# Loads of q, k and v: four chunks on odd partitions, buffers of their own, k's exp in one operation

## The chip, the cores and the metric

The kernel runs on one core of one Trainium2 chip. The metric is the time of one execution on the device in microseconds (us), lower is better. The profile's span is shorter than that time, because it begins at the first and ends at the last instruction. A run gives several timed executions and the profile of one of them. A fast execution that took 1 us or more longer than others of its kernel is called a long one below.

## The reference, cut to what matters

Linear attention with two softmaxes, then a gated feed-forward block:

```python
def _attn_ref(q, k, v):                       # each (8, 8, 576, 64) float32
    q_s = np.exp(q - np.max(q, axis=-1, keepdims=True))
    q_s = q_s / (np.sum(q_s, axis=-1, keepdims=True) + 1e-09)
    k_s = np.exp(k - np.max(k, axis=2, keepdims=True))
    k_s = k_s / (np.sum(k_s, axis=2, keepdims=True) + 1e-09)
    kv = np.einsum('bhsd,bhse->bhde', k_s, v)
    return np.einsum('bhsd,bhde->bhse', q_s, kv)

def _moe_ref(x, w_gate, w_val, w_out):        # x (4608, 512), d_ff 1536
    g = x @ w_gate
    gelu = 0.5 * g * (1.0 + erf(g * inv_sqrt2))
    return gelu * (x @ w_val) @ w_out
```

## The kernel before

A sequence of 576 rows is 64 groups of 9 rows. A partition pair shares a group: the even partition takes rows 0 to 4 (five chunks of 64 numbers per head), the odd one rows 4 to 8. Row 4 is thus loaded twice, and its copy on the odd partitions must not count: k's exp for that chunk is a second operation with a bias of -1e30 on the odd partitions, so that exp gives zero there.

```python
tiny = const.tile([P, 1], f32)
nc.vector.memset(tiny, 0.0)
kbias = const.tile([P, 1], f32)               # -1e30 on odd partitions
nc.vector.reduce_sum(kbias, ident.rearrange("p (m t) -> p t m", t=2)[:, 1, :], ...)
nc.vector.tensor_scalar(out=kbias, in0=kbias, scalar1=-1e30, scalar2=None, op0=ALU.mult)
... # ek, eq, v16, xtr, q0r, eq0r, weights follow in the same pools

def load(src, nm, b, h0, h1, n0):             # ldp: five buffers in rotation
    key = (nm, b)
    if key not in tiles:
        tiles[key] = ldp.tile([P, H, NC * D], f32, name=f"{nm}t", tag="ld")
    for t in range(2):
        nc.sync.dma_start(
            out=tiles[key][t:P:2, h0:h1, n0 * D:NC * D],
            in_=src[b, h0:h1].rearrange("h (m n) d -> m h (n d)", n=NT)[
                :, :, (4 * t + n0) * D:(4 * t + NC) * D])

... # the order of the loads, all on one queue
for src, nm, n0 in ((q, "q", 1), (k, "k", 0), (v, "v", 0)):
    load(src, nm, 0, 0, H, n0)
for c in range(NW):
    load_w_gv(c)                              # gate and value weights
for c in range(3):
    load_w_o(c)                               # output weights
load(q, "q", 1, 0, H, 0)
for c in range(3, NO):
    load_w_o(c)
```

The weights arrive as float32 in staging tiles and are cast to float16 on GpSimd. Between the feed-forward groups of a batch, the attention of the next batch is worked in by a plan: `at(batch, FI or NS, index, ...)` hangs work behind a gate/value group (FI) or an output tile (NS).

The softmax here doesn't subtract the row's maximum and nothing guards it: scores larger than these inputs give would overflow.

## Time and profile before

| | before |
|---|---|
| time, median of 3 | 324.06 us |
| the execution that was profiled | 325.62 us (span 323.8) |
| TensorE busy | 98% |
| spacing of 512-column matmul starts | 216 ns |
| v of batch 0 landed | 15.40 us |
| first feed-forward matmul | 19.07 us |
| last output weights landed | 43.91 us |

The prediction shows the page's lines for this kernel. These two rows of the windows view of the kernel before give, for 22 to 43 us and for 43 to 49 us: the length, busy time of TensorE, its weight loads, VectorE, ScalarE and GpSimd with counts, the granted clock, the DMA share and GB/s.

```profile
22.00:43.00 21.00, 21.00 (x99) 9.57 (x98) 8.20 (x12) 10.18 (x14) 13.03 (x14) 1.00 1.07 394
43.00:49.00 6.00, 5.88 (x34) 2.84 (x33) 5.27 (x10) 3.22 (x5) 3.89 (x4) 1.00 1.06 393
```

The reader is to see that the transfers run at full occupation through this whole stretch while TensorE works on what they bring. TensorE waits almost nowhere, but nothing in the row says by how much each transfer is early.

### The profile page before, as it was taken

The page shows a single profiled execution, that of the slowest core. Times are in us where ns is not written, and L with a number is a line of the kernel's source. Part 1 is how long each engine was busy: PE and PEld are TensorE (multiplying, and loading weights), DVE is VectorE, ACT ScalarE, POOL GpSimd, SP SyncE. Part 2 cuts the span into 40 slices and gives each one's busy share as a digit, 9 for nine tenths or more (in the row PEclk, how much of TensorE's full clock was granted, in tenths as well). Part 3 has the DMA queues.
Part 4 walks back from the last instruction along what each step waited for, and adds up shares of the span by engine and source line. Part 5 has one row for each costly group of instructions (what it writes and reads, how often), then busy time and mean ns, then how long its engine had stood idle before and what let it go on. Part 6 is the DMA issues. An engine that isn't in the chain of part 4 may idle for free.

```text
span 323.8 us, 4510 instructions
## 1 busy us (share of the span) xinstructions
PE 315.9 (98%) x1670; PEld 150.9 (47%) x1670; DVE 189.9 (59%) x339; ACT 142.7 (44%) x189; POOL 43.1 (13%) x58
## 2 busy tenths in 40 slices
PE   8799999999999999999999999999999999999995
PEld 3344445445445444444444444444454444444444
DVE  2654366498569758945795579647963433333431
ACT  4463476698353492238433842384321133103310
POOL 1267552303000300030003000300000000000000
PEclk9999999999999999999999999999999999999999
DMA  6999999990178004941495139512021110040002
GB/s 217 356 324 389 401 396 390 392 357 7 67 235 316 2 11 167 387 117 29 139 381 149 22 125 366 176 31 95 36 50 31 67 65 0 4 108 21 0 34 97
DMA packets 47718, 53.12 MB, mean 164 GB/s; under 512 B 11344, under 2 KB 43472, under 8 KB 47696
## 3 DMA queue, kind: packets, MB, share of 16 engines
q1 hardware_dynamic: 47552, 52.77, 47.2%
q8 instruction: 13, 0.21, 0.3%
q10 hardware_dynamic: 144, 0.07, 0.1%
q14 instruction: 9, 0.07, 0.1%
HBM read 40.76 MB, written 9.44 MB: 155 GB/s over the span
## 4 chain that ended last, share of the span: by engine, by line
PE 86%; ACT 3%; DMA 3%; issue 2%; DVE 2%; SPq 1%; POOL 0%; DVEq 0%; ACTq 0%; POOLq 0%
PE psg L305 27%; PE psv L305 27%; PE psy L349 26%; DMA vt<-in_v_dram 3%; PE pskv L200 3%; PE psx L283 2%; ACT L149 1%; SPq L103 1%; ACT eq L149 1%; PE psl L370 1%; ACT L310 1%; PE pst L226 1%; DVE kv_sb L208 0%; DVE rq L166 0%; ACT gl L310 0%
## 5 line engine op out<-in xcount | busy, mean ns | idle before, releaser
L310 ACT ACTIVATE gl<-psg 128x512 f32<-128x512 f32 x108 | 63.9, 598 | 120.2 <-PE psg L305 118.9
L312 DVE SCALAR_TENSOR_TENSOR ht<-psv,gl 128x512 f16<-128x512 f32 x108 | 73.0, 683 | 66.7 <-PE psv L305 62.3
L305 PE MATMUL psg<-xt,wg_sb 128*128 128x512 f16 x384 | 100.6, 379 | 0.1
L305 PE MATMUL psv<-xt,wv_sb 128*128 128x512 f16 x384 | 100.2, 379 | 0.1
L349 PE MATMUL psy<-wo_sb,ht 128*128 128x512 f16 x420 | 94.7, 379 | 0.0
L305 PEld LDWEIGHTS <-wv_sb 128*128 128x128 f16 x432 | 42.3, 98 | 51.8 <-issue 1.0
L349 PEld LDWEIGHTS <-ht 128*128 128x128 f16 x420 | 40.8, 98 | 47.8
L305 PEld LDWEIGHTS <-wg_sb 128*128 128x128 f16 x432 | 41.3, 98 | 46.7 <-issue 1.4
L398 DVE TENSOR_SCALAR yo<-psy 128x512 f32<-128x512 f32 x30 | 20.6, 689 | 34.6 <-PE psy L349 34.6
L125 POOL CAST v<-vt 128x640 f16<-128x640 f32 x26 | 18.3, 743 | 141.8 <-DMA vt<-in_v_dram 108.4
L166 DVE TENSOR_REDUCE rq<-eq 128x10 f32<-128x640 f16 (+1 forms) x32 | 25.3, 791 | 10.4 <-ACT eq L149 10.0
L173 DVE TENSOR_TENSOR eq<-eq,rrq 128x640 f16<-128x640 f16 (+1 forms) x28 | 23.4, 836 | 0.4
L127 ACT CAST xt<-psx 128x512 f16<-128x512 f32 x19 | 10.3, 588 | 27.3 <-PE psx L283 27.3
L149 ACT ACTIVATE eq<-qt 128x2560 f16<-128x2560 f32 (+1 forms) x9 | 18.3, 2049 | 4.2 <-DMA qt<-in_q_dram 4.1
L149 ACT ACTIVATE ek<-kt 128x2048 f16<-128x2048 f32 (+1 forms) x10 | 15.6, 1558 | 6.4 <-DMA kt<-in_k_dram 6.4
L297 PE MATMUL pswarm<-warm,ident 128*128 128x512 f16 x46 | 12.6, 435 | 1.4 <-POOL ident masks.py:199 1.4
L249 DVE STREAM_TRANSPOSE et<-eq 128x640 f16<-128x640 f16 x16 | 13.5, 845 | 0.6
L200 PE MATMUL pskv<-v,ek 128*128 128x130 f16 x160 | 11.8, 220 | 1.9 <-DVE v L129 1.9
L200 PEld LDWEIGHTS <-ek 128*128 128x128 f16 x160 | 10.3, 97 | 5.5 <-ACT v L127 2.4
L305 PE MATMUL psg<-xtr,wg_sb 128*128 128x512 f16 x48 | 12.3, 379 | 0.5 <-ACT xtr L127 0.5
L305 PE MATMUL psv<-xtr,wv_sb 128*128 128x512 f16 x48 | 12.3, 379 | 0.0
L283 PE MATMUL psx<-eqt,kv_sb 128*128 128x512 f16 x32 | 10.2, 381 | 0.3 <-DVE eqt L129 0.2
(57 smaller groups left out, 134.5 us busy)
## 6 DMA issues: line engine op xcount, KB each, us to landing
kt<-in_k_dram SPq DMA_DIRECT2D x14, 640.0 KB, 8.0
vt<-in_v_dram SPq DMA_DIRECT2D x14, 640.0 KB, 10.0
qt<-in_q_dram SPq DMA_DIRECT2D x14, 640.0 KB, 6.0
out_dram<-yo SPq DMA_DIRECT2D x14, 512.0 KB, 3.1
wost<-in_moe_w_out_dram SPq DMA_DIRECT2D x6, 512.0 KB, 7.9
wgst<-in_moe_w_gate_dram SPq DMA_DIRECT2D x5, 512.0 KB, 7.5
wvst<-in_moe_w_val_dram SPq DMA_DIRECT2D x5, 512.0 KB, 7.5
eqt<-et SPq DMA_DIRECT2D x64, 40.0 KB, 2.0
```

Source lines behind the costliest of these rows:

```text
L125: nc.gpsimd.tensor_copy(out=dst, in_=src)
L149: nc.scalar.activation(out=dst[:, c0:c1, h0 * D:h1 * D].rearrange("p n (h d) -> p h n d", d=D), in_=tiles[(nm, b)][:, h0:h1, c0 * D:c1 * D ...
L166: nc.vector.reduce_sum(rq, e, axis=mybir.AxisListType.X)
L173: (nc.gpsimd if eng == "pool" else nc.vector).tensor_tensor(out=e, in0=e, in1=rrq.unsqueeze(-1).to_broadcast((P, n, 2, D)), op=ALU.mult)
L200: nc.tensor.matmul(pskv[:, j, :], ek_b[b % 2][:, n, hp * P:(hp + 1) * P], v16_b[b % 2][:, n, 2 * hp:2 * hp + 2, 0:VW], start=(n == 0), sto ...
L249: nc.vector.transpose(out=et[:, hp].rearrange("p c (n i) -> p n c i", i=32), in_=eq_b[b % 2][:, :, hp * P:(hp + 1) * P].rearrange("p n (c ...
L283: nc.tensor.matmul(psx, st[(b, "kv", hp)].rearrange("p h e -> p (h e)"), xq(b, hp), start=True, stop=True)
L305: nc.tensor.matmul(ps, w[:, ci, fi * P:(fi + 1) * P], xt[:, ci, :], start=(ci == 0), stop=(ci == HP - 1))
L310: nc.scalar.activation(out=gl, in_=psg, func=ACTF.Gelu)
L312: nc.vector.scalar_tensor_tensor(out=ht, in0=psv, scalar=_H_SCALE, in1=gl, op0=ALU.mult, op1=ALU.mult)
L349: nc.tensor.matmul(psy, hts[fi][:, ns * P:(ns + 1) * P], wo_sb[:, fi, :], start=(fi == 0), stop=(fi == NFI - 1))
L398: nc.vector.tensor_scalar(out=yo, in0=psy, scalar1=1.0 / _H_SCALE, scalar2=None, op0=ALU.mult)
```

## The change

It saves the double load of row 4: odd partitions load four chunks. The unused fifth chunk then has to hold a constant (zero for q and v, -1e30 for k, whose exp is zero). So q, k and v get fixed buffers, filled once, and k's exp becomes one operation without a bias. Some loads and units move to other places of the plan. The core of the diff:

```diff
-    ldp = ctx.enter_context(tc.tile_pool(name="ldp", bufs=5))
...
     tiny = const.tile([P, 1], f32)
     nc.vector.memset(tiny, 0.0)
-    kbias = const.tile([P, 1], f32)
-    nc.vector.reduce_sum(kbias, ident.rearrange("p (m t) -> p t m", t=2)[:, 1, :], ...)
-    nc.vector.tensor_scalar(out=kbias, in0=kbias, scalar1=-1e30, scalar2=None, op0=ALU.mult)
...
+    ld_b = {}
+    for nm, n, fill in (("k", 2, -1e30), ("v", 1, 0.0), ("q", 2, 0.0)):
+        ld_b[nm] = []
+        for i in range(n):
+            t = const.tile([P, H, NC * D], f32, name=f"{nm}t{i}")
+            (nc.vector if i == 0 else nc.gpsimd).memset(t[:, :, 0:D], fill)
+            ld_b[nm].append(t)
...
-        for t in range(2):
+        tiles[(nm, b)] = ld_b[nm][b % len(ld_b[nm])]
+        for t, c0 in ((0, n0), (1, 1)):
             nc.sync.dma_start(
-                out=tiles[key][t:P:2, h0:h1, n0 * D:NC * D],
+                out=tiles[(nm, b)][t:P:2, h0:h1, c0 * D:NC * D],
...
-        for c0, c1 in parts if nm == "k" else ((n0, NC),):
-            nc.scalar.activation(out=..., in_=..., func=ACTF.Exp,
-                bias=kbias[:, 0:1] if c1 == 1 else 0.0)
+        nc.scalar.activation(out=..., in_=..., func=ACTF.Exp)
...
-    at(1, FI, 7, L(exp, "k", 2, 0, H, 0, ((1, NC),)), L(cast_v, 2, 0, H))
+    at(1, FI, 7, L(exp, "k", 2, 0, 4), L(cast_v, 2, 0, H))
...
-                at(b, NS, 3, L(unit_xrem, n))
+                at(b, NS, 12, L(unit_xrem, n))
...
-                mm_out(psy, hts, ns, range(NFI))
+                mm_out(psy, hts, ns, range(NFI // 2))
+                ride(b, NS, 10 + ns)
+                mm_out(psy, hts, ns, range(NFI // 2, NFI))
```

More of the change, by code (lines that the diff above doesn't have):

```diff
@@ L74 @@
     nc.vector.memset(tiny, 0.0)
-    kbias = const.tile([P, 1], f32)
-    nc.vector.reduce_sum(kbias, ident.rearrange("p (m t) -> p t m", t=2)[:, 1, :],
-                         axis=mybir.AxisListType.X)
-    nc.vector.tensor_scalar(out=kbias, in0=kbias, scalar1=-1e30, scalar2=None, op0=ALU.mult)
     ek_b, eq_b, v16_b = [], [], []
@@ L98, in load @@
     def load(src, nm, b, h0, h1, n0):
-        key = (nm, b)
-        if key not in tiles:
-            tiles[key] = ldp.tile([P, H, NC * D], f32, name=f"{nm}t", tag="ld")
-        for t in range(2):
+        tiles[(nm, b)] = ld_b[nm][b % len(ld_b[nm])]
+        for t, c0 in ((0, n0), (1, 1)):
             nc.sync.dma_start(
-                out=tiles[key][t:P:2, h0:h1, n0 * D:NC * D],
+                out=tiles[(nm, b)][t:P:2, h0:h1, c0 * D:NC * D],
                 in_=src[b, h0:h1].rearrange("h (m n) d -> m h (n d)", n=NT)[
-                    :, :, (4 * t + n0) * D:(4 * t + NC) * D])
+                    :, :, (4 * t + c0) * D:(4 * t + NC) * D])
     wst = {}
@@ L142, in cast_w_o, with exp @@
         copy_on(eng, wo_sb[:, 2 * c:2 * c + 2, :], wst[("wo", c)])
-    def exp(nm, b, h0=0, h1=H, n0=0, parts=((1, NC), (0, 1))):
+    def exp(nm, b, h0=0, h1=H, n0=0):
         dst = (ek_b if nm == "k" else eq_b)[b % 2]
-        for c0, c1 in parts if nm == "k" else ((n0, NC),):
-            nc.scalar.activation(
-                out=dst[:, c0:c1, h0 * D:h1 * D].rearrange("p n (h d) -> p h n d", d=D),
-                in_=tiles[(nm, b)][:, h0:h1, c0 * D:c1 * D].rearrange("p h (n d) -> p h n d", d=D),
-                func=ACTF.Exp, bias=kbias[:, 0:1] if c1 == 1 else 0.0)
+        nc.scalar.activation(
+            out=dst[:, n0:NC, h0 * D:h1 * D].rearrange("p n (h d) -> p h n d", d=D),
+            in_=tiles[(nm, b)][:, h0:h1, n0 * D:NC * D].rearrange("p h (n d) -> p h n d", d=D),
+            func=ACTF.Exp)
     def cast_v(b, h0, h1, eng="pool"):
@@ L414, with load_batch @@
         load_w_o(c)
-    for h0 in (0, 4):
-        load(k, "k", 1, h0, h0 + 4, 0)
-        load(v, "v", 1, h0, h0 + 4, 0)
-    def load_batch(b):
-        for src, nm in ((q, "q"), (k, "k"), (v, "v")):
+    def load_batch(b, what=((q, "q"), (k, "k"), (v, "v"))):
+        for src, nm in what:
             load(src, nm, b, 0, H, 0)
-    load_batch(2)
-    nc.sync.dma_start(out=q0r, in_=q[0].rearrange("h (m n) d -> m h (n d)", n=NT)[:, :, 0:D])
     preload(ACTF.Exp)
@@ L441 @@
     cast_v(0, 6, 8, "dve")
+    for h0 in (0, 4):
+        load(k, "k", 1, h0, h0 + 4, 0)
+        load(v, "v", 1, h0, h0 + 4, 0)
+    load_batch(2, ((q, "q"), (k, "k")))
+    nc.sync.dma_start(out=q0r, in_=q[0].rearrange("h (m n) d -> m h (n d)", n=NT)[:, :, 0:D])
     warm_pe(2)
@@ L471 @@
     at(0, NS, 5, L(unit_t, 1, 0))
-    at(0, NS, 16, L(unit_kv, 1, 0), L(cast_v, 1, 4, 8))
+    at(0, NS, 16, L(unit_kv, 1, 0), L(cast_v, 1, 4, 8), L(load_batch, 2, ((v, "v"),)))
     at(0, NS, 6, L(norm, 1, 3))
@@ L484 @@
     at(1, FI, 6, L(norm, 2, 3))
-    at(1, FI, 7, L(exp, "k", 2, 0, H, 0, ((1, NC),)), L(cast_v, 2, 0, H))
+    at(1, FI, 7, L(exp, "k", 2, 0, 4), L(cast_v, 2, 0, H))
     at(1, FI, 9, L(unit_t, 2, 0))
     at(1, FI, 10, L(unit_t, 2, 1))
-    at(1, FI, 11, L(load_batch, 3), L(exp, "k", 2, 0, H, 0, ((0, 1),)),
-       L(exp, "q", 3), L(exp, "k", 3), L(exp_rem0), L(cast_v, 3, 0, H))
+    at(1, FI, 11, L(load_batch, 3), L(exp, "k", 2, 4, 8), L(exp, "q", 3), L(exp, "k", 3), L(exp_rem0), L(cast_v, 3, 0, H))
     at(1, NS, 0, L(unit_trem, 2), L(unit_kv, 2, 0))
-    at(1, NS, 1, L(unit_x, 2, 0, "dve"), L(unit_kv, 2, 1))
+    at(1, NS, 1, L(unit_x, 2, 0, "dve"))
+    at(1, NS, 12, L(unit_kv, 2, 1))
     at(1, NS, 2, L(unit_x, 2, 1, "dve"), L(unit_x, 2, 2, "dve"))
```

## The prediction

> **What bounds the kernel now.** I read the page first, for the shares of the engines:
>
> ```profile
> PE 315.9 (98%) x1670; PEld 150.9 (47%) x1670; DVE 189.9 (59%) x339; ACT 142.7 (44%) x189; POOL 43.1 (13%) x58
> ```
>
> TensorE has work in 315.9 of 323.8 us and no other engine reaches 60%. That busy figure flatters it, since the records overlap: one 512-column matmul is recorded as 379 ns, but in the trace's order of time the starts lie 216 ns apart. So I looked for the places where starts lie further apart. Next the waits, for TensorE alone:
>
> ```profile
> PE pskv L200 <- DVE v L129: 1.9, 1, 1.9
> PE pswarm L297 <- POOL ident masks.py:199: 1.4, 1, 1.4
> PE psg L305 <- ACT xtr L127: 0.5, 1, 0.5
> PE psx L283 <- DVE eqt L129: 0.2, 1, 0.2
> ```
>
> There are four waits, 4.0 us in all, and only the first and third can concern this change. Third, the chain that ended last, cut to the first 24 us:
>
> ```profile
> 4.23 0.04 issue
> 4.27 11.13 DMA vt<-in_v_dram
> 15.40 0.03 issue
> ...
> 15.50 0.84 DVE v L129
> 16.34 0.14 issue
> 16.48 0.75 PE pskv L200 x10
> ```
>
> Up to 15.40 us the end of the kernel hangs on one thing: the second half of batch 0's v landing (issue at 4.27, landing 11.13 later). Then VectorE casts it, TensorE makes k'v, and at 19.07 us the feed-forward stream begins. From there I compared starts of neighbouring matmuls. Beyond the regular spacing there are only some 2.2 us of gaps in 300 us. The ones over 0.15 us lie at 19.1, 50.7, 52.2, 55.0, 66.5, 73.3, 89.9 and 257.2 us. Two of them bear on the change. At 73.3 us, the timelines of TensorE and of ScalarE:
>
> ```profile
> 72.66 1.02 PE L305 MATMUL psg<-xt,wg_sb 128*128 128x512 f16 x4
> 73.80 1.02 PE L305 MATMUL psv<-xt,wv_sb 128*128 128x512 f16 x4
> ```
>
> ```profile
> 68.64 1.28 ACT L149 ACT_TABLE_LOAD   x1
> 69.93 1.91 ACT L149 ACTIVATE ek<-kt 128x2048 f16<-128x2048 f32 x1
> 71.86 1.28 ACT L310 ACT_TABLE_LOAD   x1
> 73.15 1.09 ACT L310 ACTIVATE gl<-psg 128x512 f32<-128x512 f32 x2
> ```
>
> The psv group should start 0.86 us after the psg group, at 73.52; it starts at 73.80. ScalarE was away from the Gelus for 4.5 us with k's exp between two table loads. The six PSUM buffers ran full, and one came free when the Gelu of 73.15 ended (about 73.75). At 257.2 us:
>
> ```profile
> 257.13 0.28 PE L290 MATMUL psxr<-eqt,kv_sb 128*128 128x64 f16 x4
> 257.87 1.02 PE L305 MATMUL psg<-xtr,wg_sb 128*128 128x512 f16 x4 [0.46 <-ACT xtr L127]
> ```
>
> Here the remainder rows of the last batch are made and copied by ScalarE directly before the tile that reads them. The gap is 652 ns in place of 216.
>
> **What the Trainium skill says.** "DMA: Bandwidth & Descriptors", section "Why small descriptors are slow (HBM only)", gives each packet a fixed overhead besides its bytes. The trace agrees: the median packet took 27 ns with 512 bytes, 46 with 1024 and 55 with 1280. So cutting 256 bytes of 1280 saves 9 ns of 55, 16% and not 20%. "ScalarE: Activation LUTs", section "What ACT_TABLE_LOAD costs", gives an ACTIVATE with immediate bias 186 ns + 0.833 ns per element, and 93 ns more with a bias in memory. The trace has 2.34 us for 2560 elements (formula 2.32) and 1.28 us for a table load (page 1.283), so it agrees. "VectorE: DVE Perf Modes", section "Zero memsets can be issued as uint32 (trn2)", has one cycle per element for a memset; 512 elements took 0.48 us here and 256 took 0.27, which agrees.
>
> **The change part by part.**
>
> 1. Fewer bytes. An odd-partition load has 64 partitions x 8 heads = 512 packets, 32 on each of 16 DMA engines. 32 x 9 ns = 0.29 us less per tensor and batch. Ahead of v's landing lie two such loads that change (k0 and v0; q0 loaded four chunks already): 2 x 0.29 = 0.58 us. The landings of v0's odd half on the 16 engines run from 12.83 to 15.40 us, with the 15th at 14.47. One engine is late: one of its packets took 1156 ns at 6.9 us, and it works off its last v packets 52 ns apart. A lagging engine drains the same 64 changed packets, so it also gains 0.58 us, unless the odd slow packet falls otherwise. v lands near 14.82. Nothing else should then be late. The q chain on VectorE is done by 13.04. k0 also lands 0.29 earlier, near 11.8, and its two exps (part 4) end near 14.4. The gate weights follow v in the same queue and shift with it; their casts on GpSimd were 1.3 us ahead at fi 2. So the matmul start moves from 16.48 to about 15.9. On the path: -0.58 us.
>
> 2. The same saving for later tensors (about 11 x 131 KB up to batch 3) ends the busy stretch of DMA, full until about 73 us, some 3 us sooner. TensorE waits for no transfer after 19 us, so this is worth 0.
>
> 3. Constants and buffers. VectorE loses kbias (two operations, 0.36 us, plus a wait for the identity), and gets three memsets of 512 elements, estimated at 0.55 us each from the rows above; GpSimd gets two. The even half of k0 must wait for k's memset, which I put at 2.8 us: constants until 1.75, eq0r 0.48, k 0.55. It was issued at 2.24. The transfer does not notice: the first k packet ran only at 5.56, behind q, and the first packets came 1.55 us after q's issue, so an issue at 2.85 would be ready by 4.4. q0 loads chunks 1 to 4 only, which its memset doesn't touch. Worth 0.
>
> 4. k's exp as one operation. Per half tensor 1.06 + 0.49 less overlap = 1.45 us becomes 1.26 us (the cast of 1280 elements on ScalarE takes 1.26); per whole tensor 2.5 becomes 2.34. ScalarE is 44% busy, so only one place counts: at FI 7 of batch 1 the exp of 1.91 us becomes a half exp of 1.26. The Gelus return 0.65 us sooner, more than the 0.28 us gap at 73.3, which closes: -0.28 us. The other half goes behind the last Gelu of the batch (1.26 for 0.72 us), where ScalarE is wanted by nobody until 89 us.
>
> 5. Moved work. The remainder rows go from behind the fourth output tile to the middle of the third, 1.3 + 2.6 us before their reader. The gap of 652 - 216 ns closes: -0.44 us. unit_kv(2, 1) moves to mid-tile, because its exp is now later; VectorE needs about 0.8 us for its two kv_sb, and the rest of the tile is 6 x 216 ns = 1.3 us. Worth 0.
>
> Sum: -0.58 - 0.28 - 0.44 = -1.30 us. 324.06 becomes 322.8 us (-0.4%).
>
> **Rivals.**
>
> *A wait takes the place of the one removed.* v has one buffer now, so v of batch 2 cannot be asked for before GpSimd has cast v of batch 1 (51.79 to 53.17 us before), and the queue behind it (stores, batch 3) stands still meanwhile. For it: SyncE issues in order, and v2 was issued at 49.24 before. Against: v2's four casts ended at 64.87 and are read at 79.64, 15 us of slack, and an asking at 52 with 2 us of latency and 3.3 us of transfer lands near 57 to 58. It would have to be very wrong; then some 1 to 3 us lost, 324 to 326.
>
> *The memsets hold up the start.* If q0's load waited for q's own memset (the third on VectorE, near 3.8 us), every first transfer would start 3 us later: 325.5 to 326. Against: the parts touched are disjoint. Even then it stays inside 2%.
>
> *The prologue's gain is lost or doubled by the late engine.* The stall of 1156 ns is one packet of one engine. If it falls elsewhere, v can land at 14.0 (-1.5 us) or, with a second such packet, not earlier at all. That makes 321.9 to 323.4, and it is my main uncertainty.
>
> *A PSUM pair is too short at the new place of the remainder rows.* They reuse the buffer of unit_x 0, freed by VectorE (in batch 3 at 152.9 us); the new place comes at 151.88 + 1.30 = 153.2. The margin is only 0.3 us. If it fails, batches 3 to 6 lose 0.1 to 0.3 us each: up to 1 us back, 323.8.
>
> **Range and chances.** Central 322.8. All three gains hold and the late engine vanishes: 321.6. Prologue gain lost and part of the PSUM margin too: 323.9. Two per cent is 6.5 us; all gaps after 19 us plus the wait before the first k'v make 4.5 us, so faster by 2% is practically out (0.01). Slower by 2% needs a stall that I have not seen (0.01). Within: 0.98.
>
> **What would show it.** In the chain of waits the vt transfer should end near 14.8, and k'v start near 15.9 us. If it ends there and the first feed-forward matmul does not come 0.58 us sooner, the weights or ScalarE have become the limit. The row "psg waits for xtr" should be gone from TensorE's waits. In the middle of batch 1 the psg and psv starts should be 0.86 us apart, with an exp of 128x1280 near 1.26 us before. Each k load should still have its first packet directly behind q's. A wait of psxr on VectorE, of pskv on v in batch 2, or a first q issue after 3 us would make the prediction wrong.

## The result

| | before | after |
|---|---|---|
| median | 324.2 us (324.0 to 324.4, 4 executions) | 325.88 us (325.70 to 326.02, 4 executions) |
| ratio after/before | | 1.0052, 95% interval 1.0034 to 1.0069 |

The change makes the kernel 0.5% slower, and the output is correct. That is within the 2% that the prediction expected, but on the other side of zero. Here and below, a ratio is the mean time of one kernel's fast executions over the mean of the other's in the same rounds, so it isn't quite the ratio of the medians that are quoted.

The first line to look at is the DMA queue: packets, megabytes, share of the time of 16 engines. Before:

```profile
q1 hardware_dynamic: 47552, 52.77, 47.2%
```

After:

```profile
q1 hardware_dynamic: 47552, 49.75, 48.1%
```

The same number of packets carries 6% fewer bytes and keeps the engines busy for longer. Fewer bytes with more time means that the packets themselves have become slower. The windows view of the kernel after shows when that mattered (columns as above):

```profile
22.00:43.00 21.00, 20.96 (x98) 9.32 (x97) 7.46 (x11) 8.07 (x12) 12.08 (x12) 1.00 1.07 364
43.00:49.00 6.00, 4.03 (x21) 1.67 (x18) 4.24 (x8) 3.49 (x3) 3.50 (x4) 1.00 1.08 357
```

At the same share, the rate fell from 394 to 364 GB/s, and directly afterwards TensorE stood still for 2 of 6 us. The waits of TensorE in the kernel after (total us, times, longest) name who kept it:

```profile
PE psy L348 <- POOL wo_sb L126: 1.1, 2, 0.8
PE pst L225 <- POOL eq L172: 1.0, 1, 1.0
```

Neither wait is in the trace of the kernel before that the prediction read; a long execution of that kernel (a1, below) has the second, with 0.7 us. Both name GpSimd, but GpSimd is only the middle of the story. The chain of waits of the kernel after (start, length, what) leads back from the second of them to a transfer:

```profile
31.16 9.68 DMA qt<-in_q_dram
...
40.89 1.28 ACT L148
...
42.19 2.35 ACT eq L148
...
44.56 0.83 DVE rq L165
...
47.87 1.27 POOL eq L172
...
49.19 0.40 PE pst L225 x4
```

The q of batch 1 lands at 40.84 us; ScalarE's table load and exp start that moment, VectorE sums, GpSimd multiplies, and TensorE's transposes wait for it. The other wait has the same root by another way: GpSimd's casts of the output weights wait for their transfers. GpSimd's timeline in the kernel after (start, length, engine, line, what, idle time before and its releaser):

```profile
43.60 1.04 POOL L126 CAST wo_sb<-wost 128x1024 f16<-128x1024 f32 x1 [0.31 <-DMA wost<-in_moe_w_out_dram]
44.96 1.04 POOL L126 CAST wo_sb<-wost 128x1024 f16<-128x1024 f32 x1 [0.32 <-DMA wost<-in_moe_w_out_dram]
```

and TensorE beside it, where each bracket is a stall:

```profile
44.69 0.59 PE L348 MATMUL psy<-wo_sb,ht 128*128 128x512 f16 x2 [0.37 <-POOL wo_sb L126]
46.06 1.89 PE L348 MATMUL psy<-wo_sb,ht 128*128 128x512 f16 x8 [0.77 <-POOL wo_sb L126]
47.78 0.39 PE L225 MATMUL pst<-ident,eq 128*128 128x128 f16 x4
49.19 0.40 PE L225 MATMUL pst<-ident,eq 128*128 128x128 f16 x4 [1.02 <-POOL eq L172]
```

Counted as excess over the regular 216 ns between neighbouring starts, the three stalls are 0.53, 0.93 and 1.02 us, 2.49 us in all.

The two gaps that the change was to close did close. At 73 us the psg and psv groups of the kernel after start 0.86 us apart:

```profile
73.65 1.02 PE L304 MATMUL psg<-xt,wg_sb 128*128 128x512 f16 x4
74.51 1.03 PE L304 MATMUL psv<-xt,wv_sb 128*128 128x512 f16 x4
```

and the tile of the remainder rows of the last batch starts with no wait:

```profile
255.37 2.75 PE L348 MATMUL psy<-wo_sb,ht 128*128 128x512 f16 x12
257.96 1.03 PE L304 MATMUL psg<-xtr,wg_sb 128*128 128x512 f16 x4
```

So the question for the experiments was why packets became slower. The addresses in the two compiled kernels suggested an answer. The small tile `kbias` takes one 32-byte slot on each partition. It stood ahead of nearly everything else, so that without it every later tile lies 32 bytes lower. Before, the targets of the loads (q, k, v and the weights' staging tiles) began at multiples of 256 bytes, for example 93440 and 144640; after, all begin 224 past one, for example 56544 and 144608.

### The profile page after: what moved, and what is told of

It is laid out like the page before. It is cut to its first block, busy times and chain, and to the rows that moved or that the text cites. A ratio compares the mean times of both kernels' runs of the same rounds, so it can differ in the third digit from the quotient of the medians.

```text
span 323.9 us, 4499 instructions
## 1 busy us (share of the span) xinstructions
PE 316.4 (98%) x1670; PEld 150.6 (47%) x1670; DVE 191.1 (59%) x340; ACT 141.0 (44%) x180; POOL 44.8 (14%) x60
## 3 DMA queue, kind: packets, MB, share of 16 engines
q1 hardware_dynamic: 47552, 49.75, 48.1%
## 4 chain that ended last, share of the span: by engine, by line
PE 81%; DMA 8%; SPq 3%; ACT 2%; DVE 2%; issue 1%; POOL 1%; ACTq 0%; DVEq 0%; POOLq 0%
PE psy L348 26%; PE psg L304 25%; PE psv L304 24%; DMA wgst<-in_moe_w_gate_dram 5%; DMA qt<-in_q_dram 3%; PE pskv L199 2%; SPq L120 2%; PE psx L282 2%; ACT eq L148 1%; PE psl L369 1%; SPq L104 1%; ACT L148 1%; PE pst L225 1%; POOL wg_sb L126 1%; DVE rq L165 0%
## 5 line engine op out<-in xcount | busy, mean ns | idle before, releaser
L148 ACT ACTIVATE ek<-kt 128x1280 f16<-128x1280 f32 (+1 forms) x11 | 19.1, 1746 | 4.3 <-DMA kt<-in_k_dram 4.3
```

The costliest lines, as they stand in the source:

```text
L148: nc.scalar.activation(out=dst[:, n0:NC, h0 * D:h1 * D].rearrange("p n (h d) -> p h n d", d=D), in_=tiles[(nm, b)][:, h0:h1, n0 * D:NC * D ...
```

## The experiments

The theory: a DMA whose SBUF target does not start on a multiple of 256 bytes takes longer per packet, the loads up to 45 us come later by it, and TensorE waits. The rivals: the new order of loads or the fixed buffers delay them; k's exp or the moved units cost time; the difference is spread between executions. The means of packet times below are taken from the trace: 512-byte packets from 6.5 to 16 us, 1024 and 2048 bytes (weights) from 22 to 45 us. "Stalls" is the excess of TensorE's starts over 216 ns in gaps that begin between 43 and 49 us. The 0.17 us of d1 and a3 is a gap before psx that every run here has; where it begins after 49 us it isn't counted. All of these are from the profiled execution of each run; the ratio is against the kernel before in the same rounds. Runs a1 to a4 shared a chip and its rounds; so did b1 to b4, c1 to c4, and d1 to d3.

| run | targets past 256 B: q,k,v / staging | 512, 1024, 2048 B, ns | q1 lands, us | last output weights land, us | stalls, us | ratio |
|---|---|---|---|---|---|---|
| a1, before | 0 / 0 | 27.0, 46.2, 84.0 | 39.76 | 43.65 | 0.72 | 1.0010 |
| d1, before | 0 / 0 | 27.0, 46.2, 84.0 | 38.02 | 41.87 | 0.17 | one look |
| a2, after | 224 / 224 | 33.1, 50.9, 88.9 | 40.70 | 44.77 | 2.24 | 1.0059 |
| a3, after, padded | 0 / 0 | 27.0, 46.1, 84.0 | 37.18 | 41.04 | 0.17 | 0.9967 |
| b1 | 0 / 32 | 29.8, 49.9, 86.6 | 39.55 | 43.59 | 1.62 | 1.0015 |
| b2 | 224 / 0 | 27.1, 46.8, 84.4 | 38.26 | 42.05 | 0.00 | 0.9969 |
| b3 | 64 / 64 | 31.4, 50.9, 88.9 | 40.98 | 45.06 | 1.55 | 1.0031 |
| c1 | 128 / 128 | 32.8, 51.1, 89.3 | 40.44 | 44.51 | 1.65 | 1.0041 |

### The same two kernels again

The kernel before, unchanged:

> The kernel before, unchanged, for a second trace of it beside the others on one chip. Ratio 1.000. The trace that the prediction rested on was of an execution of 325.6 us, 1.5 us slower than the timed ones. If the packet of 1156 ns on one DMA engine belonged to that execution alone, v of batch 0 lands near 14.0 us here, the first feed-forward matmul comes near 17.6 us and the span is near 322.3 us. If it belongs to the kernel, v lands near 15.4 again. 1024-byte packets of the weights between 22 and 45 us should take 46 ns in the median.

324.56 us, ratio 1.0010 (0.9992 to 1.0028): no difference, as it should be. Its profiled execution was again a long one, 325.51 us, with stalls of 0.72 us between 43 and 49 us.

The kernel after, unchanged:

> The changed kernel, unchanged, on the same chip. Theory 1 (addresses): the removed kbias tile took 32 bytes of each partition, so every later tile, DMA targets included, begins 32 bytes past a multiple of 64; packets are slower whatever the chip: 1024-byte weight packets between 22 and 45 us at a mean near 51 ns against 46 in the kernel before, ratio near 1.005. Rival (this chip or its memory was slow when the trace was taken): both kernels of this call show the same packet times for the weights, and the ratio is near 1.000 or below.

326.09 us, ratio 1.0059 (1.0041 to 1.0077). The loss repeats, with the same three stalls (0.28, 0.94 and 1.02 us). It is not spread between executions.

### The addresses put back, and taken away

The kernel after with a wider `tiny`, so that all later tiles move up by the 32 bytes:

```diff
-    tiny = const.tile([P, 1], f32)
+    tiny_pad = const.tile([P, 16], f32)
+    tiny = tiny_pad[:, 0:1]
```

> The changed kernel with tiny made 64 bytes long, so that all later tiles lie on multiples of 64 again (the staging tiles at the very addresses of the kernel before); no instruction differs. Theory 1: weight packets back to 46 ns, the waits of TensorE for wo_sb and of the transposes for eq (about 2.3 us between 43 and 49 us) gone, ratio 0.995 to 0.998 against the kernel before. Rival 1 (chip): same time as the changed kernel. Rival 2 (the odd loads or the one v buffer slow the transfers): same time as the changed kernel.

323.4 us (322.99 to 323.70), ratio 0.9967 (0.9952 to 0.9982). No instruction differs from the kernel after, only addresses. The packets are as fast as before, the last output weights land 3.73 us sooner than in a2, and the stalls fall from 2.24 us to none but the common 0.17. The engines' own operands moved by the 32 bytes too, but their operations took the same time: the medians of like operations (those that occur four times or more) are within 3 ns of each other in a2 and a3. The queue's line of this run, against 48.1% in the kernel after:

```profile
q1 hardware_dynamic: 47552, 49.75, 45.5%
```

The reverse, the kernel before with its two small tiles put into one slot and nothing else changed:

```diff
-    tiny = const.tile([P, 1], f32)
+    two = const.tile([P, 2], f32)
+    tiny = two[:, 0:1]
...
-    kbias = const.tile([P, 1], f32)
+    kbias = two[:, 1:2]
```

> The kernel before with tiny and kbias in one tile, so that all later tiles lie 32 bytes past a multiple of 64 as in the changed kernel; no instruction differs. Theory 1: weight packets near 51 ns, the output weights late, ratio 1.005 to 1.010. Rivals: ratio 1.000.

327.02 us, ratio 1.0080 (1.0062 to 1.0098). The shift alone makes the old kernel 0.8% slower. The two runs multiply to 1.0080 x 0.9967 = 1.0047, and the change as a whole measured 1.0052 and 1.0059: the shift and the rest of the change explain it together.

One execution of this run, the profiled one, took 679.29 us and counts as slow, so it is in no ratio and its profile can't be read for the stalls. In it the matmuls ran at half speed throughout, although the granted clock is recorded as 1.0. Line, engine, operation, count, busy us and mean ns of one, which is 379 ns elsewhere (their starts lie 443 or 558 ns apart there, and 216 elsewhere):

```profile
L306 PE MATMUL psg<-xt,wg_sb 128*128 128x512 f16 x384 | 202.1, 678 | 0.0
```

The other five executions took 326.5 to 327.8 us. What caused the slow one stays open. Nothing in the argument rests on it.

### Which targets, and which offsets

In b1 the q, k and v buffers are on multiples of 256 and everything behind them is off (32 past), the weights' staging tiles among it; it is a3 with the last q buffer lengthened by 32 bytes. In b2 it is the other way round, q, k and v 224 past and everything behind them back on multiples, made from the kernel after by the same edit:

```diff
-            t = const.tile([P, H, NC * D], f32, name=f"{nm}t{i}")
+            if (nm, i) == ("q", 1):
+                t = const.tile([P, H * NC * D + 8], f32, name=f"{nm}t{i}")
+                t = t[:, 0:H * NC * D].rearrange("p (h x) -> p h x", h=H)
+            else:
+                t = const.tile([P, H, NC * D], f32, name=f"{nm}t{i}")
```

> The changed kernel with the q, k and v buffers on multiples of 64 and everything behind them, the weights' staging tiles too, 32 bytes past one. Theory (a DMA target off the multiple of 64 costs its packets about 5 ns each, whatever their size): the 14 + 6 weight loads of the first 45 us are slow (1024-byte packets at 51 ns, 2048 at 89), q, k and v fast; of the 3.9 us by which the last output weights landed later in the changed kernel than in the padded one, the weights' share (14 x 32 + 6 x 16 = 544 packets per engine x 5 ns = 2.7 us) stays. Nearly as slow as the changed kernel: ratio 1.002 to 1.005. If the engines' operands off the multiple of 64 were the cause, and not the DMA targets, this run could not be told from b2 by the packets.

325.13 us, ratio 1.0015 (0.9985 to 1.0044). Packets of the weights are slower by 2.6 to 3.8 ns, less than in the kernel after, and the stalls are 1.62 us.

> The opposite: q, k and v buffers 32 bytes past a multiple of 64, staging tiles and all later ones on one. Theory: q, k and v packets slow (about 192 packets per engine x 5 ns = 1 us later for v of batch 0), weight packets back at 46 ns; the last output weights land about 1.3 us later than in the padded kernel, most of the stalls near 44 to 48 us gone. Ratio 0.998 to 1.001.

323.72 us, ratio 0.9969 (0.9942 to 0.9996), the same as a3 within the intervals. Here q, k and v pay: their 1280-byte packets before 16 us took 60.2 ns in the mean, against 56.3 in a3. The q of batch 1 lands at 38.26 us, 1.08 later than in a3 (the other padded runs, c2, c3, c4 and d3 below, have it between 37.08 and 38.08), but no stall follows between 43 and 49 us. So in this kernel the staging tiles decide, since they take most of the packets ahead of the last wait.

Offsets of 64 and of 128 bytes for all of them, by a `tiny` of 32 or of 48 numbers (the edit is as in a3 but for this number):

> The padded kernel with all later tiles moved on by another 64 bytes, so that the DMA targets lie on odd multiples of 64. If 64 is the grain that counts: as the padded kernel, 46 ns for weight packets, ratio 0.995 to 0.998. If the grain is 128 or 256: slow as the changed kernel, 1.005.

325.82 us, ratio 1.0031 (1.0005 to 1.0057).

> The padded kernel with all later tiles moved on by 128 bytes: DMA targets at 128 past a multiple of 256. The run at 64 past was as slow as the changed kernel, so the grain is 128 or 256. If 256 (each 256-byte piece of a transfer then spans two 256-byte blocks of the target, one piece more per packet): weight packets at a mean near 51 ns, ratio 1.003 to 1.006. If 128: 46 ns, ratio 0.995 to 0.998.

325.92 us, ratio 1.0041 (1.0012 to 1.0070). A multiple of 64, and one of 128, doesn't help: packets cost nearly what they cost in the kernel after. Of the five offsets tried (0, 32, 64, 128, 224; 32 for the staging tiles alone) only 0 is fast.

This fits in part what the Trainium skill states in "DMA: Bandwidth & Descriptors", section "How a descriptor splits into AXI transactions": a descriptor that starts on a multiple of 256 bytes is cut into pieces of 256, and one that doesn't gets its first piece from the boundary below. By this rule, worked out here, 1024 bytes make five pieces in place of four at every offset tried but 0. The page speaks of reads and gives counts, not times. The runs varied the target and show the time: 4.4 to 6.1 ns more per packet of 512 to 2048 bytes at 64, 128 and 224 past, 2.6 to 3.8 ns at 32 past. That the extra piece is the mechanism is an inference, and it leaves open why 32 past, with as many pieces, costs less. That the address is the cause is shown, since a3 and a2 differ in nothing else.

### The bytes alone

The padded kernel with five chunks on the odd partitions again. The result is wrong (relative error 0.41), because the fifth chunk is then real data that k's exp counts twice.

```diff
-        for t, c0 in ((0, n0), (1, 1)):
+        for t, c0 in ((0, n0), (1, n0)):
```

> The padded kernel, but the odd partitions load five chunks again (the constant is overwritten, so the result is wrong on purpose). It takes away only the saving of bytes. By the prediction's part 1: v of batch 0 lands 0.58 us later than in the padded kernel and the time rises by about 0.6 us, ratio 0.998 to 0.999. If transfers have slack after 19 us, as part 2 said, nothing more; if not, the output weights (0.9 us later, three changed tensors) hold up TensorE near 43 to 48 us and it costs up to 1.5 us.

324.04 us, ratio 0.9976 (0.9946 to 1.0006). The v of batch 0 lands at 13.95 us against 13.43 in a3, 0.52 us apart, near the 0.58 that the prediction worked out. But the five padded runs that load alike (a3, c2, c3, c4 and d3) land it between 12.88 and 13.96 us, so a pair of traces can't show half a microsecond. The packets do: in a3 the median took 55 ns with 1280 bytes and 46 with 1024, as in the kernel before. The first feed-forward matmul comes at 17.68 against 17.60. Later TensorE waits 0.32 us at 46.94 us for GpSimd's `eq`, a wait that a3 doesn't have: the last output weights land at 42.66 us here and between 40.97 and 41.94 in the padded runs, which is the second case of the expectation. The executions spread over 2.2 us here and over 0.7 in a3, and the intervals overlap, so what the bytes are worth in the mean isn't settled.

### Two more looks at the kernel before

The prediction started from a long execution. These two looks were to show whether the wait for v is the rule:

> A third trace of the kernel before. If the late engine belongs to single executions: v of batch 0 lands between 13.9 and 14.6 us, all 16 engines within 1 us. If to the kernel: one engine 1 to 2 us behind again, v at 14.5 to 15.4 us.

> A fourth trace of the kernel before; as the third. Two traces that agree with each other and not with the first two would make the late engine a matter of the execution.

They took 323.85 and 324.04 us. The v of batch 0 landed at 13.71 and 14.02 us, and the first feed-forward matmul came at 17.50 and 17.68 us, against 15.40 and 19.07 in the trace that the prediction read. The chain of waits of d1 no longer goes through v:

```profile
1.57 5.08 DMA qt<-in_q_dram
...
10.47 1.05 POOL eq L173
...
11.96 1.94 PE pswarm L297 x9
...
14.96 0.69 PE pskv L200 x10
```

Here the start is set by the q chain and by TensorE's own work in order (the dummy matmuls, pswarm, that stand ahead of k'v), and v is there in time. Over all the traces one can read where v begins to count. Where it landed at 13.95 us or later, the first feed-forward matmul came 3.7 us behind it: 14.15 and 17.82 in a2, 14.55 and 18.22 in a1, 15.13 and 18.79 in b3, 15.40 and 19.07 in the prediction's trace. Where it landed sooner, the matmul came at 17.3 to 17.7 us, whatever v did. In four traces of the kernel before, v landed at 15.40, 14.55, 13.71 and 14.02 us, and only in the first two, the long executions, did TensorE wait for it (1.9 and 0.7 us).

### The exp and the casts around 70 us

In a3 the gap at 73 us was closed, but another stood at 71 us. The timelines of VectorE, GpSimd and TensorE in a3:

```profile
66.88 0.83 DVE L173 TENSOR_TENSOR eq<-eq,rrq 128x640 f16<-128x640 f16 x1
69.39 1.30 DVE L173 TENSOR_TENSOR eq<-eq,rrq 128x640 f16<-128x640 f16 x1
```

```profile
68.62 3.31 POOL L127 CAST v<-vt 128x640 f16<-128x640 f32 x4 [7.50 <-DMA vt<-in_v_dram]
```

```profile
71.34 1.02 PE L305 MATMUL psg<-xt,wg_sb 128*128 128x512 f16 x4 [0.42 <-DVE ht L312]
```

The same multiplication on VectorE takes 0.83 us alone and 1.30 beside GpSimd's cast of v of batch 3; the cast takes 3.31 us where four such casts take 2.71 elsewhere. Taken one by one, three of the four parts of the cast take 0.72 us and the third 1.31, from 69.95 to 71.26 us; it begins while the multiplication (69.39 to 70.68) runs. With faster loads this cast starts sooner and runs into VectorE's work, so that ht is late and psg waits 0.42 us. In the kernel after without the padding, v of batch 3 comes later: its cast starts at 74.73 us, when the last of these multiplications is under way (74.61, 0.82 us).

Moving that multiplication to GpSimd:

```diff
-    at(1, FI, 6, L(norm, 2, 3))
+    at(1, FI, 6, L(norm, 2, 3, "pool"))
```

> The padded kernel, with the last norm product of batch 2 on GpSimd in place of VectorE. In the padded kernel the cast of batch 3's v on GpSimd (68.62 to 71.93 us) ran beside a VectorE product, which took 1.30 us in place of 0.83, and TensorE then waited 0.43 us for ht at 70.7. GpSimd works in order, so its cast of v must now come behind the product it is given, after 72 us. Theory: the product on VectorE back at 0.83 us, the gap at 70.7 gone, 0.4 us less than the padded kernel: ratio 0.994 to 0.997. Rival (the wait has another cause, such as VectorE's load by itself): gap stays, 0.9967.

323.72 us, ratio 0.9966 (0.9942 to 0.9990): no gain over a3 (0.9967, in other rounds). The gap at 71 us is gone, and TensorE now waits 0.30 us before its start at 73.19 us, for GpSimd's multiplication. The wait only moved.

The exp of k in one whole operation, on top of c2:

```diff
-    at(1, FI, 7, L(exp, "k", 2, 0, 4), L(cast_v, 2, 0, H))
+    at(1, FI, 7, L(exp, "k", 2), L(cast_v, 2, 0, H))
...
-    at(1, FI, 11, L(load_batch, 3), L(exp, "k", 2, 4, 8), L(exp, "q", 3), ...)
+    at(1, FI, 11, L(load_batch, 3), L(exp, "q", 3), ...)
```

> The kernel of c2 with k's exp of batch 2 whole at FI 7 (2.34 us between the two table loads in place of 1.27; part 4 of the change undone). By the prediction the Gelus return 1.07 us later and TensorE waits near 71 us for a PSUM buffer: 0.28 us at least, up to 0.7 us more than c2. If VectorE and not ScalarE sets when the buffers come free there: no difference to c2.

323.54 us, ratio 0.9961 (0.9937 to 0.9985): in the time it can't be told from c2. In the trace, one matmul starts at 72.50 us, 0.89 us after the one before it: an excess of 0.67 us, where c2 has its 0.30. So halving the exp matters where the prediction said it would, by some 0.4 us. Such sizes are seen in the trace and not in the times, all the more since the time outside the span differs as well: 1.9 us in c4, 2.1 in c2.

A place for v of batch 3 where VectorE is free of such work, from a3:

```diff
-    at(1, FI, 11, L(load_batch, 3), ..., L(exp_rem0), L(cast_v, 3, 0, H))
+    at(1, FI, 11, L(load_batch, 3, ((q, "q"), (k, "k"))), ..., L(exp_rem0))
+    at(1, NS, 1, L(load_batch, 3, ((v, "v"),)), L(cast_v, 3, 0, H))
```

> The padded kernel with batch 3's v asked for behind the first store of batch 1 (near 82.7 us) and cast near 87 to 90 us, where VectorE has no 16-bit product; it is read near 92. Theory: VectorE's products near 69 to 73 us all at 0.83 us, no gap over 0.15 us between 65 and 88 us, about 0.4 us less than the padded kernel, ratio 0.993 to 0.997. Rival: a gap near 71 to 73 us stays, because VectorE's own queue is too long there; then ratio as the padded kernel, 0.9967. If v comes too late, TensorE waits on v near 92 us.

323.12 us, ratio 0.9961 (0.9946 to 0.9976), the lowest median of all, though not to be told from a3 by its interval (c4 has the same ratio). The multiplication and the cast in its trace:

```profile
69.53 0.83 DVE L173 TENSOR_TENSOR eq<-eq,rrq 128x640 f16<-128x640 f16 x1
```

```profile
89.10 2.71 POOL L127 CAST v<-vt 128x640 f16<-128x640 f32 x4 [26.86 <-DMA vt<-in_v_dram]
```

Both are back at their own lengths, and between 66 and 88 us no start of TensorE is late by 0.15 us. (One gap of 0.25 us before a psg at 65.3 us lies inside the window that the expectation named. Every kernel here has one like it.) This is the version to keep: it beats both kernels.

### The remainder rows

The padded kernel with the remainder rows back behind the fourth output tile:

```diff
-                at(b, NS, 12, L(unit_xrem, n))
+                at(b, NS, 3, L(unit_xrem, n))
```

> The padded kernel with the remainder rows again behind the fourth output tile (part 5 of the change undone). By the prediction the gap before the first psg that reads xtr is back (652 ns between starts in place of 216), so +0.44 us against the padded kernel. Rival (the PSUM pair was short at the new place and had cost something): +0.1 us or less.

323.93 us, ratio 0.9974 (0.9949 to 0.9999). TensorE's wait of the kernel before is back, with a start 652 ns after its neighbour at 255.3 us:

```profile
PE psg L305 <- ACT xtr L129: 0.5, 1, 0.5
```

It is gone in the kernel after and in a3. The ratio lies 0.0008 above that of c2 in the same rounds (the padded kernel itself wasn't in them; c2 has one multiplication on GpSimd besides); 0.44 us would make 0.0014, and the intervals are about 0.0025 to each side, so the times neither show nor exclude it. The trace does show it.

## Why the prediction was wrong

By its own parts:

**3, constants and buffers, "Worth 0".** This is the step that failed. It counted operations and waits of the constants, and these were right: k's even half was issued at 3.03 us (2.85 predicted), and the first 1280-byte packet ran at 5.66 against 5.56 us, with no effect. (Its memsets on VectorE took 0.48 us each and not 0.55; 0.48 was in the rows that the estimate came from.) It didn't ask where the remaining tiles would lie once `kbias` was gone. The shift by 32 bytes cost 2.6 us in the kernel before (1.0080) and turned the gain into a loss. The sum can be followed. Up to the last output weights an engine works off 544 packets of weights and 256 of q, k and v: 800 packets at about 5 ns more are 4.0 us by this estimate, and a2 against a3 shows 3.73. The change's fewer bytes take 3 x 0.29 = 0.87 us off that for k and v of batch 0 and q of batch 1, and a3 against d1 shows 0.83; since the five padded runs spread over 0.97 us here, that close a match is luck. So the last output weights land 44.77 - 41.87 = 2.90 us later in a2 than in d1, and TensorE's stalls there grow by 2.24 us (the 0.17 of d1 is the gap that a2 has too).

**2, later loads, "TensorE waits for no transfer after 19 us, so this is worth 0".** The reading was right for a gain and wrong as a picture of the slack. Count from the first feed-forward matmul to the landing of the last output weights. In the runs without a stall (a3, b2, c2, c3, c4, d1, d2, d3) that takes 23.4 to 24.4 us. It takes 24.8 us with 0.12 us of stalls (the prediction's trace), 25.0 with 0.32 (b4), 25.4 with 0.72 (a1), 26.2 to 26.4 with 1.55 to 1.65 (b1, b3, c1), 27.0 with 2.24 (a2) and 27.4 with 2.49 (the kernel after). So by these runs some 0.4 us of delay were free in d1 (24.4), and nearly all beyond that comes back as a stall.

**1, fewer bytes, "On the path: -0.58 us".** The saving per packet was right (55 and 46 ns). That it is on the path was read from an execution that took 1.56 us longer than the median. In ordinary executions v is there in time or just in time, since it counts only from about 14 us on. First feed-forward matmuls came at 17.50 and 17.68 us before (d1, d2), and at 17.50 and 17.82 after.

**4, k's exp, "-0.28 us".** The gap at 73.3 us closed, with a half exp of 1.27 us before it. In the padded kernel 0.42 us was lost again at 71 us to the cast beside VectorE's work, until d3 took that away.

**5, moved work, "-0.44 us".** Right: the wait of psg for xtr is gone in the kernel after and comes back in c3.

From d1 to a2 the sum is: start +0.31, stalls +2.24, exp -0.28, remainder rows -0.44, together +1.8 us; the spans differ by 323.8 - 322.0 = 1.8. Put against the prediction, the terms 4 and 5 stand, term 1 falls away, and the missing term is +2.24 us from the addresses.

Of the rivals, none was it. Batch 2's v was issued at 53.69 us and landed at 63.55, later than the 57 to 58 worked out, yet no wait of TensorE followed. The memsets held nothing up. No wait of psxr for a buffer is in any trace. The third, the late engine, was rightly named as a doubt, but as a doubt on the size of a gain and not on whether the trace was typical. What makes a load late in some executions is open; the four traces of the kernel before show that it happens and not why.

With the addresses put back, the change is worth 0.33% (a3) or 0.39% (d3), that is 1.1 to 1.3 us by the ratios, close to the 1.30 predicted. That is partly chance, since term 1 wasn't to be had in ordinary executions. Fastest against fastest of the same rounds, the times are only 0.90 us (322.99 against 323.89, a3) and 0.88 us (322.89 against 323.77, d3) apart; the rest of the mean comes from the spread of the executions, wider in the kernel before (1.39 and 1.16 us) than in a3 and d3 (0.71 and 0.90). On the other side, some 0.3 us of the change's gain is lost outside the span, where the time is 2.1 us longer than the span and not 1.8. What takes it no run shows.

## What to carry to other kernels

Look at the addresses of DMA targets in SBUF whenever a tile is added or removed, however small, and keep large targets on multiples of 256 bytes; if a change moves bytes and DMA time in opposite directions, look there first. Before a term is taken from a chain of waits, compare the time of the profiled execution with the timed ones. An absent wait says nothing of the margin: work out how long before its use each transfer lands, since a delay of 3 us cost 2.5 here.

## What the Trainium skill lacked or had wrong

- "DMA: Bandwidth & Descriptors", section "How a descriptor splits into AXI transactions", counts pieces for reads and gives no time, and says nothing of an SBUF target. Here a target 224 bytes past a multiple of 256 raised the mean packet from 27.0 to 33.1 ns (512 bytes), from 46.1 to 50.9 (1024) and from 84.0 to 88.9 (2048), and offsets of 32, 64 and 128 were slow too. Moves of 320 bytes within SBUF took 22.1 to 22.5 ns in runs whose source and target tiles began on multiples of 64, and 24.3 to 25.1 where they began 32 or 224 past a multiple of 256.
- "SBUF — State Buffer", section "Operand start alignment", is about legality alone and says that its runs timed nothing. A line on speed is missing: all these addresses are legal, and the shift of 32 bytes cost 0.8% of a whole kernel (1.0080, 1.0062 to 1.0098).
